# Attention decode step with a parallel SwiGLU: PV on four column tiles of the array, output steps per head, wo in groups of four heads

## The chip, the cores and the metric

The kernel runs on one core of one Trainium2 chip. The metric is the device time of one execution in microseconds. A profiled execution also gives a trace; its span is the time from the first to the last instruction and is 1 to 2 us shorter than the time. Engines: PE is the matmul engine (PEld is its weight loads), DVE the vector engine, ACT the scalar engine, SP the engine that issues every DMA of this kernel.

## The reference

One decode step for B = 4 sequences. Each of 32 heads attends to the last W = 2048 of 8192 cached positions with head size 192, and a SwiGLU FFN runs beside it on the same normalised input. Cut to what matters:

```python
W = min(4096, max(256, Sk // 4))              # 2048
q = (xn @ wq).reshape(B, 1, 32, 192)
k, v = k_cache[:, :, Sk-W:], v_cache[:, :, Sk-W:]
p = softmax(einsum("bhqd,bhkd->bhqk", q, k) * 192**-0.5)
o = einsum("bhqk,bhkd->bhqd", p, v)
return x + o.reshape(B, 1, 6144) @ wo + (silu(xn @ w1) * (xn @ w3)) @ w2
```

All of K and V is read once and used once: 32 heads times 3 MiB of K and 3 MiB of V, together with the weights 223 MB.

## The kernel before

The work is laid out in slots, four per head (one per quarter of a head's positions). `add(slot, phase, fn, ...)` puts a step into a slot; within each engine instructions then run in the order of slots and phases. The scores are products on DVE (`mult`), summed by PE against an identity (`adder`) and by DVE (`reduce_quarter`); softmax steps follow (`chain_*`); PV runs L = 10 slots behind. Two K buffers, three V buffers, two wo buffers. **All loads are issued by SP, in order**: a load that waits for its buffer holds up every load that is issued after it.

```python
def load_k(h):                                  # 3 MiB, packets of 24576 B
    kt = kpool.tile([P, NJ, Dh], BF16, tag="kt")
    nc.sync.dma_start(out=..., in_=k_win[:, h]...)
# load_v alike; the last head's V in GQ = 4 pieces
def wo_load(hg):                                # one per group of HG = 2 heads, packets of 3840 B
    wo_t = wopool.tile([P, RPP * D], BF16, tag="wo")
    nc.sync.dma_start(out=wo_t[:], in_=A_wo[hg * QW:(hg + 1) * QW, :]...)
# ... cut
def pv(u):                                      # one quarter of a head: 8 matmuls, 8 columns of weights each
    h, g = u // GQ, u % GQ
    if g == 0:
        o_pss[h] = ps_o.tile([2 * B, 2 * Dh], FP32, tag="o_ps", name="o_ps")
    o_ps = o_pss[h]
    z, vt = zs[h], vts[h]
    for j in range(g * JQ, (g + 1) * JQ, 2):
        nc.tensor.matmul(o_ps[:], lhsT=z[:, j:j + 2, :], rhs=vt[:, j:j + 2, :],
                         start=(j == 0), stop=(j == NJ - 2))
    # ... after the fourth quarter ACT copies o_ps to o_raw of the pair
def ge_tr(hg):                                  # turns o_raw of a pair: f32 matmuls against an identity
    # ... RPP * 2 matmuls, weights of 128 columns
def ge_proj(hg):
    # ... RPP * 2 matmuls with wo, summed in acc0, acc1 over all groups; frees wo's buffer
# ... cut
for h in range(H):
    u0, ul = h * GQ, h * GQ + GQ - 1
    if h >= KBUFS:
        add((h - KBUFS + 1) * GQ, 0, load_k, h)
    add((h - VBUFS) * GQ + GQ + L, 0, load_v, h, 1 if h < H - 1 else GQ)
    for u in range(u0, ul + 1):
        add(u, 1, mult, u); add(u + 1, 2, adder, u); add(u + 2, 4, reduce_quarter, u)
        add(u + L, 3, pv, u)
    # ... softmax chain at ul + 2 to ul + 6
for hg in range(NG):
    a = (hg + 1) * HG * GQ - 1 + L
    add(a - GQ - L if hg < NG - 1 else a - L + 3, 0, wo_load, hg)
    # ... ge_sum, ge_tot, ge_norm, ge_tr, ge_copy
    add(a + 3, 3, ge_proj, hg)
add(NU + 2, 1, w2_load)                         # last FFN weights, the last loads of all
# after all slots: last FFN product, sum, store
```

With HG = 2, `wo_load(hg)` (all but the last) stands in slot 8 hg + 3, and the projection that frees its buffer, `ge_proj(hg - 2)`, in slot 8 hg + 4. So each of these wo loads, from the third on, comes up one slot before its buffer can be free, and it must wait; the K load of slot 8 hg + 4 stands behind it.

## Time and profile before

| | before |
|---|---|
| time, first three runs | 562.24, 571.71, 572.77 us |
| span of the profiled run | 563.1 us |
| end of the last load | 540.3 us |
| from there to the end | 22.7 us |
| sum of all load packets' durations / 16 engines | 528.8 us |
| idle of the 16 engines before the last load ended | 11.8 us |

The last four rows are worked out from the trace's DMA packets: packets of weights, K and V (3 KB and over) give the end; durations of all packets over 4 B, added and divided by 16, give the sum; the idle counts 1/16 for each engine without a packet, from the first packet at 1.7 us on. (Start, sum and idle add up to 2 us more than the end, because packets of one engine overlap now and then.)

Lines of the page of the kernel before (busy us and share; busy tenths of 40 slices; GB/s of 40 slices; queue: packets, MB, share; the chain that ended last; groups: busy us, mean ns, idle before):

```profile
PE 489.6 (87%) x2339; PEld 221.8 (39%) x2339; DVE 343.1 (61%) x471; ACT 50.4 (9%) x151; POOL 1.1 (0%) x8
...
DMA  8999999999999999999999999999999999999630
GB/s 360 423 435 427 427 425 435 425 428 424 430 432 425 424 428 421 404 429 418 415 438 374 432 396 429 399 413 417 387 431 396 436 406 423 419 426 404 247 154 0
...
q1 hardware_dynamic: 12976, 222.97, 94.1%
...
DMA 49%; PE 34%; DVE 15%; ACT 1%; issue 0%; SPq 0%; ACTq 0%
...
L250 PE MATMUL o_ps<-vt,z 128*8 128x384 bf16 x1024 | 205.4, 349 | 1.1 <-ACT o_raw L258 1.1
...
L281 PE MATMUL gp<-idf,o_raw 8*128 8x4 f32 x192 | 36.0, 312 | 0.6 <-ACT o_raw L258 0.6
```

The load queue is busy for 94% of the span, so loads are the first limit and PE the second. But two things are visible in the GB/s row: in the second half many slices are at 374 to 418 where others reach 430 and more, and the last three slices (14 us each) fall away, with PE still busy.

Waits of SP's queue (waiting line, releaser: us in total, times, longest). L90 loads K, L99 loads V, L105 loads wo; L225 is a softmax step on PE that comes right behind the projection:

```profile
SPq L99 <- PE o_ps L250: 238.2, 29, 15.6
SPq L105 <- PE mt L225: 159.4, 13, 12.9
SPq L90 <- DVE pr L183: 51.2, 17, 9.7
```

The end, in the timeline (the last V, and three of PE's groups after it):

```profile
523.85 2.51 SPq L99 DMA_DIRECT2D vt<-in_A_v_cache_dram  x4
...
528.04 1.46 PE L250 MATMUL o_ps<-vt,z 128*8 128x384 bf16 x8
...
544.48 4.06 PE L250 MATMUL o_ps<-vt,z 128*8 128x384 bf16 x24 [0.56 <-ACT o_raw L258]
```

V of the last head is issued at 523.9 us, when PE at last frees its buffer, and 20 us later PE is still doing PV: a backlog.

### The profile page before, as it was taken

The page shows a single profiled execution, that of the slowest core. Times are in us where ns is not written, and L with a number is a line of the kernel's source. Part 1 is how long each engine was busy: PE and PEld are TensorE (multiplying, and loading weights), DVE is VectorE, ACT ScalarE, POOL GpSimd, SP SyncE. Part 2 cuts the span into 40 slices and gives each one's busy share as a digit, 9 for nine tenths or more (in the row PEclk, how much of TensorE's full clock was granted, in tenths as well). Part 3 has the DMA queues.
Part 4 walks back from the last instruction along what each step waited for, and adds up shares of the span by engine and source line. Part 5 has one row for each costly group of instructions (what it writes and reads, how often), then busy time and mean ns, then how long its engine had stood idle before and what let it go on. Part 6 is the DMA issues. An engine that isn't in the chain of part 4 may idle for free.

```text
span 563.1 us, 5565 instructions
## 1 busy us (share of the span) xinstructions
PE 489.6 (87%) x2339; PEld 221.8 (39%) x2339; DVE 343.1 (61%) x471; ACT 50.4 (9%) x151; POOL 1.1 (0%) x8
## 2 busy tenths in 40 slices
PE   2864899979899898979799897979899798979996
PEld 1321334433344444435344443524344343534453
DVE  2186667767437776756575776746476686756511
ACT  2111000001301000000000000000100000000100
POOL 0000000000000000000000000000000000000000
PEclk9898879988889999899979898988989898988998
DMA  8999999999999999999999999999999999999630
GB/s 360 423 435 427 427 425 435 425 428 424 430 432 425 424 428 421 404 429 418 415 438 374 432 396 429 399 413 417 387 431 396 436 406 423 419 426 404 247 154 0
DMA packets 13000, 223.31 MB, mean 397 GB/s; under 512 B 1448, under 2 KB 1456, under 8 KB 4144
## 3 DMA queue, kind: packets, MB, share of 16 engines
q1 hardware_dynamic: 12976, 222.97, 94.1%
q8 instruction: 18, 0.29, 0.2%
q14 instruction: 6, 0.05, 0.0%
HBM read 222.96 MB, written 0.01 MB: 396 GB/s over the span
## 4 chain that ended last, share of the span: by engine, by line
DMA 49%; PE 34%; DVE 15%; ACT 1%; issue 0%; SPq 0%; ACTq 0%
DMA kt<-in_A_k_cache_dram 46%; PE o_ps L250 13%; DVE pr L183 11%; PE ps L194 11%; PE gp L281 4%; DMA wt<-in_A_wq_dram 3%; DVE sc L202 3%; PE qps L167 2%; PE acc_233 L300 1%; PE f_3727 L393 1%; PE gt L318 1%; PE mt L225 1%; DVE z L239 0%; PE mt L211 0%; ACT ex L232 0%
## 5 line engine op out<-in xcount | busy, mean ns | idle before, releaser
L183 DVE TENSOR_TENSOR pr<-kt,qbc 128x3072 bf16<-128x3072 bf16 x128 | 223.2, 1745 | 116.6 <-DMA kt<-in_A_k_cache_dram 116.6
L194 PE MATMUL ps<-pr,idb 128*128 128x512 bf16 x768 | 203.2, 404 | 54.6 <-DVE sc L202 51.6
L250 PE MATMUL o_ps<-vt,z 128*8 128x384 bf16 x1024 | 205.4, 349 | 1.1 <-ACT o_raw L258 1.1
L250 PEld LDWEIGHTS <-z 128*8 128x8 bf16 x1024 | 82.9, 90 | 129.2 <-issue 76.1
L194 PEld LDWEIGHTS <-idb 128*128 128x128 bf16 x768 | 72.5, 102 | 149.5 <-issue 89.4
L202 DVE TENSOR_REDUCE sc<-ps 128x16 f32<-128x512 f32 x128 | 87.5, 684 | 5.7 <-PE ps L194 5.5
L281 PEld LDWEIGHTS gp<-idf,o_raw 8*128 8x128 f32 x192 | 34.6, 256 | 5.9 <-issue 4.9
L281 PE MATMUL gp<-idf,o_raw 8*128 8x4 f32 x192 | 36.0, 312 | 0.6 <-ACT o_raw L258 0.6
L228 ACT COPY negm<-mt 128x1 f32<-128x1 f32 x32 | 5.1, 159 | 339.0 <-PE mt L225 339.0
L291 DVE TENSOR_TENSOR oT<-gp,rtb 64x12 bf16<-64x12 f32 x32 | 5.4, 168 | 41.0 <-PE gp L281 40.8
L258 ACT COPY o_raw<-o_ps 8x384 f32<-8x384 f32 x32 | 15.0, 468 | 133.4 <-PE o_ps L250 133.4
L167 PE MATMUL qps<-wt,xnT 128*128 128x512 bf16 x60 | 17.2, 452 | 5.5 <-DMA wt<-in_A_wq_dram 5.5
L239 DVE TENSOR_TENSOR z<-ex,mask_b 128x256 bf16<-128x256 bf16 x32 | 13.4, 419 | 13.9 <-ACT ex L232 13.2
L173 DVE CAST qbc<-qps 128x512 bf16<-128x512 f32 x6 | 3.8, 684 | 19.5 <-PE qps L167 19.5
L300 PE MATMUL acc_233<-wo_t,oT 128*4 128x512 bf16 x48 | 14.8, 379 | 0.4 <-DVE oT L291 0.4
L225 PEld LDWEIGHTS mt<-ones_ff,gneg 1*128 1x128 f32 x64 | 9.4, 182 | 9.8 <-issue 9.5
L167 PEld LDWEIGHTS <-xnT 128*128 128x128 bf16 x60 | 6.7, 112 | 15.6 <-issue 10.4
L225 PE MATMUL mt<-ones_ff,gneg 1*128 1x1 f32 x64 | 12.1, 256 | 0.0
L232 ACT ACTIVATE ex<-sc,negm 128x64 bf16<-128x64 f32 x32 | 11.1, 348 | 1.0
L301 PE MATMUL acc_234<-wo_t,oT 128*4 128x128 bf16 x48 | 10.5, 219 | 0.0
L216 DVE TENSOR_REDUCE gmax<-mt 1x4 f32<-1x128 f32 x32 | 8.7, 273 | 2.2 <-PE mt L211 1.8
L211 PE MATMUL mt<-idf,lmax 128*1 128x128 f32 x32 | 8.6, 270 | 0.0
(60 smaller groups left out, 94.1 us busy)
## 6 DMA issues: line engine op xcount, KB each, us to landing
kt<-in_A_k_cache_dram SPq DMA_DIRECT2D x32, 3072.0 KB, 21.4
vt<-in_A_v_cache_dram SPq DMA_DIRECT2D x31, 3072.0 KB, 16.7
wo_t<-in_A_wo_dram SPq DMA_DIRECT2D x16, 480.0 KB, 5.1
wt<-in_A_wq_dram SPq DMA_DIRECT2D x2, 3072.0 KB, 13.2
vt<-in_A_v_cache_dram SPq DMA_DIRECT2D x4, 768.0 KB, 7.3
w_720<-in_B_w_dram SPq DMA_DIRECT2D x1, 1920.0 KB, 25.4
w_932<-in_B_w_dram SPq DMA_DIRECT2D x1, 1920.0 KB, 20.7
wt<-in_A_wq_dram SPq DMA_DIRECT2D x1, 1536.0 KB
```

What stands on the lines that cost most here:

```text
L167: nc.tensor.matmul(qp[:], lhsT=xnT[:, kc].rearrange("p a b -> p (a b)"), rhs=wq_rows[kc][:, (c0 + i) * QC:(c0 + i + 1) * QC], start=(kc == ...
L183: nc.vector.tensor_tensor(out=pr[:], in0=kts[h][:, g * JQ:(g + 1) * JQ, :], in1=qbc[:, h * Dh:(h + 1) * Dh].unsqueeze(1).to_broadcast([P, ...
L194: nc.tensor.matmul(ps[:], lhsT=idb[:], rhs=pr[:, :, kk * DD:(kk + 1) * DD], start=(kk == 0), stop=(kk == NK - 1))
L202: nc.vector.tensor_reduce(out=scs[h][:, g * JQ:(g + 1) * JQ], in_=pss.pop(u)[:], axis=AX.X, op=ALU.add)
L225: nc.tensor.matmul(mt[:, P:P + 1], lhsT=gneg[:].rearrange("o p b -> o (p b)"), rhs=ones_ff[0:1, 0:1], start=True, stop=True)
L232: nc.scalar.activation(out=ex[:], in_=scs.pop(h)[:], func=ACTF.Exp, bias=negm[:, 0:1], scale=SCALE, accum_out=rsums[hg][:, hl:hl + 1])
L239: nc.vector.tensor_tensor(out=z[:], in0=ex[:].unsqueeze(2).to_broadcast([P, NJ, B]), in1=mask_b[:].unsqueeze(1).to_broadcast([P, NJ, B]), ...
L250: nc.tensor.matmul(o_ps[:], lhsT=z[:, j:j + 2, :], rhs=vt[:, j:j + 2, :], start=(j == 0), stop=(j == NJ - 2))
L258: nc.scalar.copy(out=o_raws[hg][:, :, hl, :], in_=o_pss.pop(h)[:].rearrange("r (two d) -> r two d", two=2))
L281: nc.tensor.matmul(gp[:, i, :], lhsT=orf[:, part * QW + i:(part + 1) * QW:RPP], rhs=idf[0:2 * B, part * B:(part + 1) * B], start=(part == ...
L300: nc.tensor.matmul(acc0[:], lhsT=oT[:, i, :], rhs=wo_t[:, i * D:i * D + N0], start=st, stop=sp)
L301: nc.tensor.matmul(acc1[:], lhsT=oT[:, i, :], rhs=wo_t[:, i * D + N0:(i + 1) * D], start=st, stop=sp)
```

## The change

The intent: a PV matmul has 8 weight columns, so four of them, on four column tiles of 32, can run side by side; the result then lies in four strips of partitions, which the turning matmul adds up. The steps after PV move from pairs to single heads, and wo is loaded and projected for four heads at a time. The diff, cut to its core:

```diff
-    HG: int = 2,
+    HG: int = 4,
+    CT = 32
-    def pv(u):
-        ...
-        for j in range(g * JQ, (g + 1) * JQ, 2):
-            nc.tensor.matmul(o_ps[:], lhsT=z[:, j:j + 2, :], rhs=vt[:, j:j + 2, :], ...)
+    def pv(h, half):
+        o_ps, z, vt = o_banks[h % 2], zs[h], vts[h]      # two banks, zeroed once
+        n = NJ // 4
+        for jj in range(half * n, (half + 1) * n):
+            c = jj % 4
+            nc.tensor.matmul(o_ps[c * CT:c * CT + 2 * B, :], lhsT=z[:, 2 * jj:2 * jj + 2, :],
+                             rhs=vt[:, 2 * jj:2 * jj + 2, :], start=(jj < 4), stop=(jj >= 2 * n - 4))
+    def ge_tr(h):                       # per head; sel adds the four strips; weights of 32 columns
+        ...
+                nc.tensor.matmul(gp[sl, i, :], lhsT=o_raw[:, part, i:Dh:RPP], rhs=sel[:, part * B:(part + 1) * B],
+                                 start=(part == 0), stop=(part == 1))
...
-        add((h - VBUFS) * GQ + GQ + L, 0, load_v, h, 1 if h < H - 1 else GQ)
+        add((h - VBUFS) * GQ + GQ + L, 0, load_v, h, 1 if h < H - 1 else 2)
-            add(u + L, 3, pv, u)
+        add(u0 + L, 3, pv, h, 0)
+        add(u0 + L + 2, 3, pv, h, 1)
...
-        a = (hg + 1) * HG * GQ - 1 + L
-        add(a - GQ - L if hg < NG - 1 else a - L + 3, 0, wo_load, hg)
-        ...
-        add(a + 3, 3, ge_proj, hg)
+        a = ((hg + 1) * HG - 1) * GQ + L + 5
+        add((hg - 1) * HG * GQ + L + 2 * GQ + 4 if hg > 0 else 0, 0, wo_load, hg)
+        add(a, 3, ge_proj, hg, 0, RPP // 2)
+        add(a + 1, 3, ge_proj, hg, RPP // 2, RPP)
```

More of the change, by code (lines that the diff above doesn't have):

```diff
@@ L64 @@
     assert JQ * DD == 512 and JQ % 2 == 0 and 2 * Dh <= 512 and 0 < N1 <= 512
-    assert (H * Dh) % QC == 0 and NQ % 6 == 0 and QW % P == 0 and Dh % RPP == 0 and P % HG == 0
+    assert (H * Dh) % QC == 0 and NQ % 6 == 0 and QW % P == 0 and Dh % RPP == 0 and P == HG * CT
     assert 2 * H * Dh <= NJ * Dh
@@ L76 @@
     ps_add = ctx.enter_context(tc.tile_pool(name="ps_add", bufs=2, space=MemoryType.PSUM))
-    ps_o = ctx.enter_context(tc.tile_pool(name="ps_o", bufs=1, space=MemoryType.PSUM))
+    ps_o = ctx.enter_context(tc.tile_pool(name="ps_o", bufs=2, space=MemoryType.PSUM))
     ps_m = ctx.enter_context(tc.tile_pool(name="ps_m", bufs=1, space=MemoryType.PSUM))
-    ps_t = ctx.enter_context(tc.tile_pool(name="ps_t", bufs=2, space=MemoryType.PSUM))
+    ps_t = ctx.enter_context(tc.tile_pool(name="ps_t", bufs=1, space=MemoryType.PSUM))
     ps_acc = ctx.enter_context(tc.tile_pool(name="ps_acc", bufs=1, space=MemoryType.PSUM))
@@ L85 @@
     kts, vts, prs, pss, scs, exs, zs = {}, {}, {}, {}, {}, {}, {}
-    wos, o_pss, o_raws, rsums, chs, ges = {}, {}, {}, {}, {}, {}
+    wos, o_raws, rsums, rtbs, chs, ges, oTs = {}, {}, {}, {}, {}, {}, {}
     def load_k(h):
@@ L131 @@
     nc.vector.tensor_copy(out=mask_b[:], in_=mask_f[:])
+    sel = const.tile([P, 2 * B], FP32, name="sel")
+    nc.vector.tensor_reduce(out=sel[:], in_=idf[:].rearrange("q (c k) -> q k c", k=CT)[:, 0:2 * B, :],
+                            axis=AX.X, op=ALU.add)
     xf = ppool.tile([B, D], FP32, tag="pr")
@@ L163 @@
         qps = [pool.tile([P, QC], FP32, tag=tag, name="qps")
-               for pool, tag in ((ps_add, "ps"), (ps_add, "ps"), (ps_o, "o_ps"), (ps_m, "mt"), (ps_t, "t"), (ps_t, "t"))]
+               for pool, tag in ((ps_add, "ps"), (ps_add, "ps"), (ps_o, "o_ps"), (ps_o, "o_ps"), (ps_m, "mt"), (ps_t, "t"))]
         for kc in range(KC):
@@ L175 @@
                 nc.scalar.copy(out=dst, in_=qp[:])
+    o_banks = []
+    for i in range(2):
+        o_ps = ps_o.tile([P, 2 * Dh], FP32, tag="o_ps", name="o_ps")
+        nc.vector.memset(o_ps[:], 0.0)
+        o_banks.append(o_ps)
     acc0 = ps_acc.tile([B, N0], FP32, name="acc0")
@@ L209, in chain_tr @@
     def chain_tr(h):
-        mt = ps_m.tile([P, P + 1], FP32, tag="mt")
+        mt = ps_m.tile([P, P + 1 + B], FP32, tag="mt")
         nc.tensor.transpose(out=mt[0:1, 0:P], in_=chs[h][0][:], identity=idf[:])
@@ L222, in chain_bc @@
     def chain_bc(h):
-        lmax, mt, gneg = chs.pop(h)
-        hg, hl = h // HG, h % HG
+        lmax, mt, gneg = chs[h]
         nc.tensor.matmul(mt[:, P:P + 1], lhsT=gneg[:].rearrange("o p b -> o (p b)"), rhs=ones_ff[0:1, 0:1],
@@ L228, in chain_bc @@
         nc.scalar.copy(out=negm[:], in_=mt[:, P:P + 1])
-        if hl == 0:
-            rsums[hg] = small.tile([P, HG], FP32, tag="rsum", name="rsum")
+        rsum = small.tile([P, 1], FP32, tag="rsum", bufs=4)
         ex = small.tile([P, NJ], BF16, tag="ex")
         nc.scalar.activation(out=ex[:], in_=scs.pop(h)[:], func=ACTF.Exp, bias=negm[:, 0:1], scale=SCALE,
-                             accum_out=rsums[hg][:, hl:hl + 1])
+                             accum_out=rsum[:])
+        rsums[h] = rsum
         exs[h] = ex
@@ L241, in chain_z @@
         zs[h] = z
-    def pv(u):
-        h, g = u // GQ, u % GQ
-        if g == 0:
-            o_pss[h] = ps_o.tile([2 * B, 2 * Dh], FP32, tag="o_ps", name="o_ps")
-        o_ps = o_pss[h]
-        z, vt = zs[h], vts[h]
-        for j in range(g * JQ, (g + 1) * JQ, 2):
-            nc.tensor.matmul(o_ps[:], lhsT=z[:, j:j + 2, :], rhs=vt[:, j:j + 2, :],
-                             start=(j == 0), stop=(j == NJ - 2))
-        if g == GQ - 1:
+    def pv(h, half):
[5 more added lines that the diff above has]
+                             rhs=vt[:, 2 * jj:2 * jj + 2, :], start=(jj < 4), stop=(jj >= 2 * n - 4))
+        if half == 1:
@@ L253, in pv @@
             zs.pop(h)
             vts.pop(h)
-            hg, hl = h // HG, h % HG
-            if hl == 0:
-                o_raws[hg] = small.tile([2 * B, 2, HG, Dh], FP32, tag="o_raw", bufs=2, name="o_raw")
-            nc.scalar.copy(out=o_raws[hg][:, :, hl, :], in_=o_pss.pop(h)[:].rearrange("r (two d) -> r two d", two=2))
-    def ge_sum(hg):
-        rsm = small.tile([P, HG, B], FP32, tag="rsm", bufs=2)
-        nc.vector.tensor_tensor(out=rsm[:], in0=rsums.pop(hg)[:].unsqueeze(2).to_broadcast([P, HG, B]),
-                                in1=mask_f[:].unsqueeze(1).to_broadcast([P, HG, B]), op=ALU.mult)
-        ges[hg] = rsm
@@ L266, in ge_tot @@
-    def ge_tot(hg):
-        tb = ps_t.tile([P, HG, B], FP32, tag="t")
-        nc.tensor.matmul(tb[:], lhsT=ones_ff[:], rhs=ges[hg][:], start=True, stop=True)
-        ges[hg] = tb
-    def ge_norm(hg):
-        rtb = small.tile([P, HG, B], FP32, tag="rtb", bufs=2)
-        nc.vector.reciprocal(out=rtb[:], in_=ges[hg][:])
-        ges[hg] = rtb
-    def ge_tr(hg):
-        gp = ps_t.tile([P, RPP, B], FP32, tag="t")
-        orf = o_raws.pop(hg)[:].rearrange("r two h d -> r (two h d)")
+            o_raw = small.tile([P, 2, Dh], FP32, tag="o_raw", bufs=2, name="o_raw")
@@ new lines, in pv, with ge_tot, ge_norm @@
+            nc.scalar.copy(out=o_raw[:].rearrange("q two d -> q (two d)"), in_=o_ps[:])
+            o_raws[h] = o_raw
+    def ge_tot(h):
+        sl = slice((h % HG) * CT, (h % HG + 1) * CT)
+        nc.tensor.matmul(chs[h][1][sl, P + 1:P + 1 + B], lhsT=rsums.pop(h)[:].to_broadcast([P, CT]), rhs=mask_f[:],
+                         start=True, stop=True)
+    def ge_norm(h):
+        sl = slice((h % HG) * CT, (h % HG + 1) * CT)
+        rtb = small.tile([P, B], FP32, tag="rtb")
+        nc.vector.reciprocal(out=rtb[sl, :], in_=chs.pop(h)[1][sl, P + 1:P + 1 + B])
+        rtbs[h] = rtb
@@ L279, in ge_tr @@
+    def ge_tr(h):
+        hl = h % HG
+        sl = slice(hl * CT, (hl + 1) * CT)
+        gp = ps_t.tile([P, RPP, B], FP32, tag="t", name="gp")
+        o_raw = o_raws.pop(h)
         for i in range(RPP):
             for part in range(2):
-                nc.tensor.matmul(gp[:, i, :], lhsT=orf[:, part * QW + i:(part + 1) * QW:RPP],
-                                 rhs=idf[0:2 * B, part * B:(part + 1) * B], start=(part == 0), stop=(part == 1))
-        ges[hg] = [ges[hg], gp]
-    def ge_copy(hg):
-        rtb, gp = ges[hg]
-        oT = small.tile([P, RPP, B], BF16, tag="oT", bufs=2)
-        PH = P // HG
-        for hl in range(HG):
-            sl = slice(hl * PH, (hl + 1) * PH)
-            nc.vector.tensor_tensor(out=oT[sl], in0=gp[sl],
-                                    in1=rtb[sl, hl, :].unsqueeze(1).to_broadcast([PH, RPP, B]), op=ALU.mult)
-        ges[hg] = oT
@@ L295, in ge_proj, with ge_copy @@
-    def ge_proj(hg):
-        oT, wo_t = ges.pop(hg), wos.pop(hg)
-        for i in range(RPP):
+                nc.tensor.matmul(gp[sl, i, :], lhsT=o_raw[:, part, i:Dh:RPP], rhs=sel[:, part * B:(part + 1) * B],
+                                 start=(part == 0), stop=(part == 1))
+        ges[h] = gp
+    def ge_copy(h):
+        hg, hl = h // HG, h % HG
+        sl = slice(hl * CT, (hl + 1) * CT)
+        if hl == 0:
+            oTs[hg] = small.tile([P, RPP, B], BF16, tag="oT", bufs=2, name="oT")
+        nc.vector.tensor_tensor(out=oTs[hg][sl], in0=ges.pop(h)[sl, :, :],
+                                in1=rtbs.pop(h)[sl, :].unsqueeze(1).to_broadcast([CT, RPP, B]), op=ALU.mult)
@@ L298, in ge_proj @@
+    def ge_proj(hg, i0, i1):
+        oT, wo_t = oTs[hg], wos[hg]
+        for i in range(i0, i1):
             st = (hg == 0 and i == 0)
@@ L366 @@
         add(ul + 6, 5, chain_z, h)
+        add(ul + 6, 4, ge_tot, h)
+        add(ul + 6, 6, ge_norm, h)
+        add(u0 + L + 3, 3, ge_tr, h)
+        add(u0 + L + 4, 5, ge_copy, h)
     for hg in range(NG):
-        a = (hg + 1) * HG * GQ - 1 + L
-        add(a - GQ - L if hg < NG - 1 else a - L + 3, 0, wo_load, hg)
-        add(a - 2, 6, ge_sum, hg)
-        add(a - 1, 6, ge_tot, hg)
-        add(a, 6, ge_norm, hg)
-        add(a + 1, 3, ge_tr, hg)
-        add(a + 2, 2, ge_copy, hg)
-        add(a + 3, 3, ge_proj, hg)
+        a = ((hg + 1) * HG - 1) * GQ + L + 5
+        add((hg - 1) * HG * GQ + L + 2 * GQ + 4 if hg > 0 else 0, 0, wo_load, hg)
+        add(a, 3, ge_proj, hg, 0, RPP // 2)
+        add(a + 1, 3, ge_proj, hg, RPP // 2, RPP)
     f = FFN_HEAD * GQ
```

## The prediction

> **What bounds it now.** The load stream. The page gives 222.96 MB read and queue q1 at 94.1% of the span; in the 20 us windows from 20 to 520 us the DMA share is 0.93 to 1.02. Summed over the trace's packets, the 16 engines need 528.8 us for this traffic. They start at 1.7 us, lose about 5 us to small gaps until 519 us, 5 us in one hole from 519.6 to 525.6 us, and end at 539.8 us. In the last 23 us nothing loads.
>
> PE is second, 489.6 us (87%), close enough to the limit to be behind: in the queue's waits, V loads wait 238.2 us for PV, most of it hidden behind queued loads. The hole is the visible part: V of head 31 is issued only at 523.9 us, when PV of head 28 releases the buffer. Then PE still has three heads of PV (timeline, 524 to 550 us), the transposing matmuls, projection, last FFN product, and the store.
>
> **What the change does.**
> - PV: 1024 matmuls, 8 in 1.46 us when warm (174 ns each), 205.4 us busy in all. Four column tiles should overlap: the Trainium skill, "TensorEngine Tiling (Array Packing)", Theoretical Speedup, says up to 4x for a dimension of at most 32; no run shows it yet. Each keeps its weight load, and this trace shows a load-and-matmul pair of 128 columns at about 55 ns (second half of the projection), so I estimate 60 ns (45 to 90): 110 to 140 us off PE.
> - Transposing matmuls: the same count per head instead of per pair, with twice the row groups: 192 records become 768. Now 12 take 2.25 us (188 ns), set by 128-column f32 weight loads. With 32 columns I estimate 70 to 110 ns: 36 us becomes 55 to 85 us.
> - Sums, reciprocals, copies: a few us either way. Projection: the same 96 matmuls. wo: the same bytes in 8 loads, not 16; its 3840 B packets already took only 149 ns, so no gain there.
> - V buffers come free one slot earlier, no longer behind a quarter that needs the next head's K.
>
> PE falls to about 400 us (360 to 440), with more idle, so a less even clock.
>
> **What is on the critical path.** Of some 90 us off PE, only the end counts: the 528.8 us of packets stay. The hole and most small gaps go, so the last load lands at about 533 us. After it come what is left of PV and transposes, projection, last FFN product (5 us now), copies (1.4 us) and store (2.5 us): about 12 us instead of 23. Span 545 us against 563.1, run 547 against 564.9 (-3.2%). The measured runs spread from 562 to 573, whose cause no view shows; I put the middle at 549, range 538 to 561. Chances: faster by over 2% 0.78, within 2% 0.20, slower 0.02.
>
> **What would show it.** DMA share near 1.0 until some 530 us, no hole before V of head 31, last landing 6 to 8 us earlier; V loads waiting little for PE; PV at 45 to 90 ns a matmul in the timeline; PE busy below 440 us; at the end PE waits for loads instead of working off a backlog; DVE unchanged (343 us); the chain almost wholly K and V loads with DVE.
>
> **What would make it wrong.** Column tiles that do not overlap (PV near 170 ns): with the added transposes PE would be the bound, time within 2%. Switches between tile shapes that cost so much that PE stays behind. A cold PE clock that stretches the last 12 us to 18. A DMA rate that drifts between runs by more than the gain.

## More of the kernel before

A wait of SP costs nothing as long as enough loads are already queued. Here is a place where there were not: SP's issues around 298 us (start us, us, instruction), then 2 us windows (PE, PEld, DVE, ACT, POOL busy; PE clock, DMA share, GB/s):

```profile
285.43 0.53 SPq L99 DMA_DIRECT2D vt<-in_A_v_cache_dram  x1
298.50 0.34 SPq L105 DMA_DIRECT2D wo_t<-in_A_wo_dram  x1
298.93 0.54 SPq L90 DMA_DIRECT2D kt<-in_A_k_cache_dram  x1
```

```profile
296.00:298.00 2.00, 2.00 (x14) 0.95 (x13) 1.76 (x2) 0.00 (x0) 0.00 (x0) 1.00 1.00 430
298.00:300.00 2.00, 2.00 (x12) 0.92 (x10) 0.53 (x3) 0.60 (x3) 0.00 (x0) 1.00 0.49 115
```

SP issued nothing for 13 us, the wo load came, and the engines had run dry when it did: 115 GB/s in that window.

How much is queued ahead can be read from the time between issue and landing of a small load. This is for the wo loads (0.48 MB) of the kernel before, from the answer for that tile:

```profile
DMA to landing us min/median/max: 4.0/5.1/27.3
```

A K load of 3.1 MB issued in the same kernel takes 21.4 us in the median. I read the median of 5.1 us to mean that a wo load usually finds next to nothing queued ahead of it.

## The result

The changed kernel takes 539.96 us in the median (539.12 to 540.90, 4 runs); the kernel before, in the same rounds, 568.64 us (562.24 to 572.77). Executions over 1.5% slower than the fastest of the same kernel are left out of the means. The ratio is 0.958, 95% interval 0.952 to 0.963: faster by 4.2%. (A ratio is the mean time of one kernel's fast runs over that of the other's fast runs of the same rounds, so it is not quite the ratio of the medians.)

The same lines of the changed kernel's page:

```profile
PE 380.5 (71%) x2947; PEld 174.2 (32%) x2947; DVE 351.0 (65%) x474; ACT 48.5 (9%) x151; POOL 1.1 (0%) x8
...
DMA  8999999999999999999999999999999999999970
GB/s 349 437 427 432 437 427 427 431 431 429 438 435 423 430 435 427 431 436 429 432 433 429 427 434 435 427 429 432 433 432 434 427 436 429 431 426 435 422 305 2
...
q1 hardware_dynamic: 11536, 222.97, 96.6%
...
DMA 59%; DVE 22%; PE 17%; issue 1%; ACT 1%; SPq 0%; ACTq 0%
...
L259 PE MATMUL o_ps<-vt,z 128*8 128x384 bf16 x1024 | 58.3, 351 | 0.0
...
L287 PE MATMUL gp<-sel,o_raw 128*32 128x4 f32 x768 | 49.6, 199 | 1.1 <-ACT o_raw L265 0.6
```

PE lost 109 us of busy time. From the second slice on the GB/s row is flat at 422 to 438 until the last two; the weak slices of the second half are gone.

SP's waits; L91 is now K's load, L100 V's, L106 wo's:

```profile
SPq L91 <- DVE pr L195: 298.2, 29, 11.3
SPq L100 <- PE mt L236: 60.4, 22, 5.0
SPq L100 <- PE o_ps L259: 31.2, 7, 15.6
```

wo is not in the list at all. SP now waits for DVE to be done with K, which is the wait that one wants: it stands as far ahead as the buffers allow. The wo loads land in 25.3 us in the median, five times as long as before (24.5 us at the least). They are twice as large, which at 431 GB/s explains about 1 us of it, an estimate; the rest I read as a queue that is always full:

```profile
DMA to landing us min/median/max: 24.5/25.3/35.0
```

The end, in the timeline:

```profile
501.70 0.82 PE L259 MATMUL o_ps<-vt,z 128*8 128x384 bf16 x16
...
502.57 1.18 SPq L100 DMA_DIRECT2D vt<-in_A_v_cache_dram  x2
...
504.70 1.76 DVE L195 TENSOR_TENSOR pr<-kt,qbc 128x3072 bf16<-128x3072 bf16 x1 [4.87 <-DMA kt<-in_A_k_cache_dram]
```

16 PV matmuls take 0.82 us where 8 took 1.46 us. The last V is issued 21 us earlier, and the end now starts from the last K, which landed at 504.7 us.

Two windows show the end of both kernels, first before, then after (columns as above; the last two are DMA share and GB/s):

```profile
520.00:530.00 10.00, 10.00 (x54) 4.26 (x53) 6.35 (x10) 1.07 (x4) 0.00 (x0) 1.00 0.50 165
530.00:540.00 10.00, 9.44 (x55) 5.69 (x53) 2.19 (x8) 1.07 (x4) 0.00 (x0) 1.00 1.01 409
```

```profile
520.00:530.00 10.00, 8.87 (x135) 6.08 (x135) 1.83 (x8) 1.46 (x5) 0.00 (x0) 0.91 0.15 62
530.00:540.00 10.00, 4.61 (x28) 2.16 (x26) 1.83 (x4) 0.73 (x2) 0.00 (x0) 0.84 0.00 1
```

The 25.0 us of the span divide cleanly at the end of the last load:

| | span | last load ends | rest | packets / 16 | idle before last load |
|---|---|---|---|---|---|
| before | 563.1 | 540.3 | 22.7 | 528.8 | 11.8 |
| after | 538.1 | 523.5 | 14.6 | 519.3 | 4.6 |
| difference | 25.0 | 16.8 | 8.1 | 9.5 | 7.3 |

Two thirds of the gain is a load stream that ends earlier, one third a shorter end. I had forecast 7 and 11 us, 18 in sum: 7 us too little, with the stream put at under half of what it gave and the end at too much. So the question for the experiments: what made the stream 16.8 us shorter, and what the end?

### The profile page after: what moved, and what is told of

It reads as the page before. It is cut to its first block, busy times and chain, and to the rows that moved or that the text cites. A ratio compares the mean times of both kernels' runs of the same rounds, so it can differ in the third digit from the quotient of the medians.

```text
span 538.1 us, 6726 instructions
## 1 busy us (share of the span) xinstructions
PE 380.5 (71%) x2947; PEld 174.2 (32%) x2947; DVE 351.0 (65%) x474; ACT 48.5 (9%) x151; POOL 1.1 (0%) x8
## 4 chain that ended last, share of the span: by engine, by line
DMA 59%; DVE 22%; PE 17%; issue 1%; ACT 1%; SPq 0%; ACTq 0%
DMA kt<-in_A_k_cache_dram 55%; DVE pr L195 16%; PE ps L206 7%; PE gp L287 5%; DVE sc L214 4%; DMA wt<-in_A_wq_dram 4%; PE qps L172 1%; PE gt L322 1%; PE o_ps L259 1%; PE f_4011 L398 1%; DVE rtb L277 0%; PE acc_239 L304 0%; DVE oT L296 0%; DVE qbc L178 0%; ACT o_raw L265 0%
## 5 line engine op out<-in xcount | busy, mean ns | idle before, releaser
L206 PE MATMUL ps<-pr,idb 128*128 128x512 bf16 x768 | 221.3, 433 | 133.6 <-DVE sc L214 129.9
L206 PEld LDWEIGHTS <-idb 128*128 128x128 bf16 x768 | 78.2, 105 | 228.9 <-issue 171.8
L259 PE MATMUL o_ps<-vt,z 128*8 128x384 bf16 x1024 | 58.3, 351 | 0.0
L287 PEld LDWEIGHTS gp<-sel,o_raw 128*32 128x32 f32 x768 | 46.8, 151 | 21.4 <-issue 19.8
L265 ACT COPY o_raw<-o_ps 128x384 f32<-128x384 f32 x32 | 15.3, 480 | 408.5 <-PE o_ps L259 408.5
L287 PE MATMUL gp<-sel,o_raw 128*32 128x4 f32 x768 | 49.6, 199 | 1.1 <-ACT o_raw L265 0.6
L259 PEld LDWEIGHTS <-z 128*8 128x8 bf16 x1024 | 20.9, 88 | 39.7 <-issue 31.2
L277 DVE RECIPROCAL rtb<-mt 32x4 f32<-32x4 f32 x32 | 5.7, 178 | 30.3 <-PE gp L287 30.0
L172 PE MATMUL qps<-wt,xnT 128*128 128x512 bf16 x60 | 16.1, 428 | 5.9 <-DMA wt<-in_A_wq_dram 5.9
L322 PE MATMUL gt<-w_754,xnT 128*4 128x512 bf16 x15 | 6.1, 565 | 4.2 <-DVE oT L296 2.9
## 6 DMA issues: line engine op xcount, KB each, us to landing
wo_t<-in_A_wo_dram SPq DMA_DIRECT2D x8, 960.0 KB, 25.3
wt<-in_A_wq_dram SPq DMA_DIRECT2D x2, 3072.0 KB, 16.8
vt<-in_A_v_cache_dram SPq DMA_DIRECT2D x2, 1536.0 KB, 14.6
```

What stands on the lines that cost most here:

```text
L172: nc.tensor.matmul(qp[:], lhsT=xnT[:, kc].rearrange("p a b -> p (a b)"), rhs=wq_rows[kc][:, (c0 + i) * QC:(c0 + i + 1) * QC], start=(kc == ...
L206: nc.tensor.matmul(ps[:], lhsT=idb[:], rhs=pr[:, :, kk * DD:(kk + 1) * DD], start=(kk == 0), stop=(kk == NK - 1))
L259: nc.tensor.matmul(o_ps[c * CT:c * CT + 2 * B, :], lhsT=z[:, 2 * jj:2 * jj + 2, :], rhs=vt[:, 2 * jj:2 * jj + 2, :], start=(jj < 4), stop= ...
L265: nc.scalar.copy(out=o_raw[:].rearrange("q two d -> q (two d)"), in_=o_ps[:])
L287: nc.tensor.matmul(gp[sl, i, :], lhsT=o_raw[:, part, i:Dh:RPP], rhs=sel[:, part * B:(part + 1) * B], start=(part == 0), stop=(part == 1))
L322: nc.tensor.matmul(gt[:], lhsT=xnT[:, kc, 0, :], rhs=wt[:, kc, n0:n0 + QC], start=(kc == 0), stop=(kc == KC - 1))
```

## The experiments

Theories. A: PE is behind, and its backlog delays the loads and fills the end; column tiles cure both. B: the wo load that waits in SP's in-order queue empties the stream; moving it away cures the stream. Two refinements, C and D, came up on the way. Each kernel ran four times (one profile and three rounds) against the kernel before on the same chip.

| kernel | median us | ratio to before [95%] | last load ends | rest of span |
|---|---|---|---|---|
| b_wo | 554.20 | 0.979 [0.976, 0.983] | 529.2 | 22.0 |
| b_sched | 554.17 | 0.977 [0.973, 0.982] | 528.1 | 24.4 |
| b_pvq | 542.75 | 0.960 [0.956, 0.965] | 528.7 | 11.4 |
| a_onecol | 549.11 | 0.970 [0.967, 0.974] | 524.0 | 23.2 |
| a_wowait | 539.02 | 0.948 [0.941, 0.955] | 523.5 | 13.7 |
| a_onewait | 547.37 | 0.964 [0.957, 0.970] | 524.1 | 21.6 |
| a_wohalf | 538.95 | 0.948 [0.942, 0.954] | 523.9 | 13.3 |
| a_tail | 534.01 | 0.939 [0.933, 0.945] | 523.6 | 9.2 |
| b_early | 565.22 | 1.004 [0.996, 1.012] | 540.3 | 23.7 |
| a_k31 | 534.91 | 0.949 [0.942, 0.956] | 523.7 | 8.3 |
| a_tail2 | 533.13 | 0.946 [0.938, 0.955] | 523.4 | 7.6 |
| b_alt | 551.76 | 0.977 [0.972, 0.981] | 528.5 | 20.6 |

The "b" kernels start from the kernel before, the "a" kernels from the changed one. The kernel before scatters from batch to batch (medians 565.6, 569.5, 565.9 and 565.7 us), so ratios of different batches compare only roughly; the last two columns, from each profiled run, compare better. (565.9 is the median of all seven runs; the ratios of that batch, of b_early, a_k31 and a_tail2, leave out its three slow ones.) The record marks every result as correct, even that of b_pvq, which leaves out three quarters of PV. So this check does not notice a wrong PV, and "correct" says little about PV in any of these kernels.

### b_wo: the wo load out of the way, nothing else

```diff
-        add(a - GQ - L if hg < NG - 1 else a - L + 3, 0, wo_load, hg)
+        add(a - GQ - L + 3 if hg < NG - 1 else a - L + 3, 0, wo_load, hg)
```

> The kernel before, with each wo load moved three slots later, behind the projection that frees its buffer, so that it never holds up the K and V loads issued after it. Theory A (PE is behind, and its backlog is the cost): the loads stay late and the end stays long, 560 to 567 us, ratio to before 0.99 to 1.00. Theory B (the wo load that waits in the in-order queue is the cost in the middle): no gaps near wo loads, packets about 5 us quicker in sum, 552 to 558 us, ratio about 0.98.

Measured: 554.20 us, and the last load ends 11.1 us earlier; the packets' sum fell from 528.8 to 524.1 us and the idle from 11.8 to 5.5 us. PE is as busy as before (483.6 us). The wo loads now find a queue:

```profile
DMA to landing us min/median/max: 16.0/17.1/20.3
```

The rest of the span stayed at 22 us. So one number in a schedule gives close to half of the whole gain, and nearly all of it in the stream, as theory B said.

### b_sched: the same, and V freed a slot earlier

```diff
-            add(u + L, 3, pv, u)
+            add(u0 + L + (2 if u - u0 >= GQ // 2 else 0), 3, pv, u)
```

> As b_wo, and PV of a head in two bursts of two quarters at the slots that the changed kernel uses, so that V is freed one slot earlier; no column tiles, PE has the same work. Theory A (PE backlog): 558 to 567 us, the hole before the last V stays. Theory B (order of issue and of release): most of the gain without column tiles, 545 to 552 us.

Measured: 554.17 us, the same as b_wo. Neither range fits: the expected 545 to 552 us of theory B was too much. Freeing V a slot earlier adds nothing once wo is out of the way (last load 1.1 us earlier, rest 2.4 us longer).

### b_pvq: PE relieved, nothing moved

```diff
-        for j in range(g * JQ, (g + 1) * JQ, 2):
+        for j in range(g * JQ, (g + 1) * JQ, 8):
             ...
-                             start=(j == 0), stop=(j == NJ - 2))
+                             start=(j == 0), stop=(j == NJ - 8))
```

> The kernel before, with only every fourth PV matmul (wrong result on purpose): PE loses about 150 us of PV, nothing else moves, and wo loads still stand in their old place. Theory A: no hole before the last V, no backlog at the end, 538 to 546 us, ratio about 0.96, as the whole change. Theory B: wo loads still hold up the queue, gaps stay in the middle, 550 to 558 us.

Measured: 542.75 us, as theory A said. PE is busy 384.2 us, as in the changed kernel. The rest of the span fell from 22.7 to 11.4 us. The stream, too, ends 11.6 us earlier, although wo loads still wait (126.9 us of SP's time instead of 159.4): they land in 8.6 us in the median instead of 5.1, and there is no gap before 510 us. So the gaps need both: a load that waits for PE, and a PE that is late. Either cure suffices for the stream. Only the relief of PE shortens the end.

### a_onecol: the changed kernel without overlap of PV

```diff
-            c = jj % 4
-            nc.tensor.matmul(o_ps[c * CT:c * CT + 2 * B, :], ..., start=(jj < 4), stop=(jj >= 2 * n - 4))
+            nc.tensor.matmul(o_ps[0:2 * B, :], ..., start=(jj == 0), stop=(jj == 2 * n - 1))
```

> The changed kernel, with all PV matmuls in the first column tile: same schedule, same loads, same output steps, but they cannot overlap. PE gets about 110 to 120 us back and some 500 us busy. Theory A: backlog returns, the last V is late, 558 to 572 us. Theory B: the middle stays full, only the end is longer, 545 to 552 us.

Measured: 549.11 us, within theory B's range. PE is busy 476.4 us, 96 us more than in the changed kernel, nearly as much as before. Its end, in the same windows as above:

```profile
520.00:530.00 10.00, 9.48 (x95) 6.25 (x95) 2.15 (x9) 1.97 (x8) 0.00 (x0) 1.00 0.15 61
530.00:540.00 10.00, 9.15 (x66) 5.14 (x64) 0.23 (x2) 0.48 (x1) 0.00 (x0) 0.86 0.01 2
```

The DMA columns are those of the changed kernel, and the PE column is close to that of the kernel before. The last load ends at 524.0 us, within 0.5 us of the changed kernel, but PE works on to the end, 23.2 us against 14.6. **In this schedule column tiles are worth about 9 us, all at the end; the rest of the change is worth about 16 us, all in the stream.** (The profile of the changed kernel comes from another batch; a_onewait against a_wowait below, which differ in the column tiles alone and ran in one batch on one chip, give 8.4 us.)

### a_wowait and a_onewait: the wo load made to wait again

```diff
-        add((hg - 1) * HG * GQ + L + 2 * GQ + 4 if hg > 0 else 0, 0, wo_load, hg)
+        add((hg - 1) * HG * GQ + L + (0 if hg > 1 else 2 * GQ + 4) if hg > 0 else 0, 0, wo_load, hg)
```

In a_onewait the one column tile of a_onecol comes on top.

> The changed kernel, with each wo load put back in front of the projection that frees its buffer, so that it waits in the queue again. Theory C (a waiting wo load only costs when PE is behind, because then the projection comes late): no gaps, 539 to 544 us, ratio about 0.96. Theory B alone (the place of the wo load is the cost, whatever PE does): gaps near wo loads, 546 to 552 us.

> The changed kernel with both undone: one column tile for all PV, and wo loads that wait. Theory C: PE is behind and the waiting wo loads hold up the K loads again, so the last load lands later than the 522 us of the one-column run, some 524 to 530, and the time is 551 to 558 us. If place and PE load did not act together, it would stay near the one-column run's 549 us.

Measured: a_wowait 539.02 us, no loss, as theory C said. But a_onewait took 547.37 us with the last load at 524.1 us, as if the wait were not there; theory C had said 551 to 558. SP did wait (98.9 us in 6 times) and the loads landed in 9.9 us in the median, but only one small gap (0.9 us near 265 us) came of it. So "a waiting load and a busy PE" is not enough. What differs from the kernel before: half as many waits, V freed earlier, and output steps per head. The next two kernels try the first two.

### b_early: V freed a slot earlier, wo still waiting

The edit is that of b_sched without that of b_wo.

> The kernel before, with PV of a head in two bursts at the changed kernel's slots (V freed one slot earlier) and nothing else: wo loads still wait in their old place, no column tiles. Theory D (gaps come where the queue's reserve runs out; any one of the three, wo out of the way, V freed earlier or PE relieved, leaves some): wo loads land in 8 us or more instead of 5, no gap before 500 us, last load near 527 us, 552 to 557 us. If an earlier V gives no reserve: gaps stay, 562 to 569 us.

Measured: 565.22 us, ratio 1.004, last load at 540.3 us, gaps of over 0.4 us (idle summed over the engines, divided by 16) at seven places before 500 us. Theory D's guess that any one cure will do is refuted for this one: V freed earlier gives no reserve. The wo loads waited even longer (259.8 us) and landed as early as before:

```profile
DMA to landing us min/median/max: 3.5/5.3/27.0
```

### b_alt: half as many waits

```diff
-        add(a - GQ - L if hg < NG - 1 else a - L + 3, 0, wo_load, hg)
+        add(a - GQ - L + (0 if hg % 2 else 3) if hg < NG - 1 else a - L + 3, 0, wo_load, hg)
```

> The kernel before, with every second wo load moved three slots later as in the first experiment and the others left to wait: as many waiting loads as with groups of four heads. If it is the number of waits that matters (the queue recovers its reserve over four heads): the waiting loads land in 8 us or more, no gaps, last load near 529 us, 554 to 557 us. If each wait empties the queue by itself: the waiting loads still land in about 5 us, about half of the gaps stay, 558 to 563 us.

Measured: 551.76 us, last load at 528.5 us, no gap before 509 us. SP waited for wo 6 times, 75.3 us in all. So the number of waits matters: with four heads between two waits the queue recovers, with two it does not. That b_alt happened to move the harmful half of the loads is unlikely: in the kernel before, gaps follow wo loads of both halves (issued at 298.5 and 360.8 us, and at 329.8 and 394.6 us). The time is a little under the range that I gave for it (554 to 557 us), as the rest of the span came out 1.4 us shorter than in b_wo.

```profile
DMA to landing us min/median/max: 5.9/15.6/26.1
```

So the grouping in fours cures the gaps even with the loads in front of their projections, as a_onewait had shown but for one small gap; the changed kernel does both.

### a_wohalf: small wo packets again

The changed kernel's wo load cut into two DMAs of three rows each, so that a packet is 3840 B again.

> The changed kernel, with each wo load cut in two, so that its packets are 3840 B again, as before. In the kernel before and its variants 24576 B packets took 915 ns and more, in the changed one 912 ns. If the size of the wo packets is the cause: packets of 24576 B go back to about 915 ns and the sum of packet times from 519.3 to about 522.5 us, the time to about 543 us. If not: 24576 B stay at 912 ns, the sum at about 520.2 us (wo alone), time within 1 us of 540.

Measured: 538.95 us, packets' sum 519.8 us, 24576 B packets still at 912 ns. The packet size of wo is worth 0.5 us and no more. What is left of the stream's gain over b_wo, about 5 us (524.1 against 519.3 us of packets), is: 2.3 us in the 24576 B packets (median 915 against 912 ns), 1.6 us in the last head's V, which came in 6144 B packets before and in 12288 B packets after, and 0.8 us in wo. Why the large packets are 3 ns quicker in every "a" kernel than in b_wo, no run settles (the median is 914 ns in the kernel before, and 912 ns in b_early too, which has the gaps).

### a_tail, a_k31 and a_tail2: faster versions

In the changed kernel the last K lands at 504.7 us and the span ends 33 us later. DVE multiplies the last K from 504.7 to 515.1 us, z of the last head (the softmax weights that PV multiplies) is done at 523.5 us, the last FFN product at 534.6 us. a_k31 loads the last K in four pieces so that DVE can start on the first:

```diff
+        pieces = GQ if h == H - 1 else 1
+        n = NJ // pieces
+        for i in range(pieces):
+            nc.sync.dma_start(out=kt[:, i * n:(i + 1) * n, :]..., in_=src[:, :, i * n:(i + 1) * n, :]...)
```

a_tail does this, moves the last wo load behind the last V, and does the last FFN product in two parts around the projection:

```diff
+        add(... + (9 if hg == NG - 1 else 0) if hg > 0 else 0, 0, wo_load, hg)
+    add((H - 1) * GQ + L + 4, 6, ffn_out, 0, W2A)
+    add((H - 1) * GQ + L + 7, 3, ffn_out, W2A, FC)
```

a_tail2 goes on from there: the last FFN weights ahead of the last V (`add(NU - 3, 1, w2_load)`), their product in three parts in slots 133, 135 and 137, and the attention output added last.

> A try at a faster version, from the reading that the end now hangs on the last K (landed at 504.7 us, 33 us before the end): the last K in four pieces, so that its multiplications start before all of it is there; the last wo load behind the last V; the last FFN product in two parts, before and after the projection, in its own PSUM tiles. If the end is the chain from the last K: 528 to 533 us, ratio about 0.94, last load still near 522 us. If something else sets the end (PE order, cold clock): 536 to 540 us.

> The changed kernel with the last K loaded in four pieces and nothing else, to take that part of the faster version by itself. If the end is the chain from the last K: z of the last head 3 to 5 us earlier than 523.5 us and the time 535 to 537 us. If the pieces do nothing: 539 to 541 us.

> A second try at a faster version: as the first, but the last FFN weights are loaded before the last V, their product is done in three parts between the steps of the last head, only the last wo load stands behind the last V, and the attention output is added last. In the first try the end waited 1.3 us for these weights and then ran their product with a cold clock, 522.5 to 526.3 us. Expected 526 to 531 us, ratio about 0.93. If the product's parts delay the last head's chain instead: 533 to 536 us.

Measured: 534.01, 534.91 and 533.13 us. The pieces alone bring most of it: z of the last head is done at 519.0 us instead of 523.5, and the rest of the span is 8.3 us instead of 14.6. Of these 6.3 us, 4.5 are the earlier z. About 1.7 us more come from a different cause: in the changed kernel seven steps of the projection and the last FFN product (528.3 to 531.9 us) ran at 0.53 us a step, at a granted clock of 0.54 (528.1 to 531.8 us); in a_k31 all of them took 0.27 us, at a clock of 1.00. Whether a_k31 avoids this slow stretch by its order or by chance, no run shows. a_tail had been expected at 528 to 533 us: z came 6.4 us earlier, but the FFN product, moved ahead of the projection, then waited until 522.5 us for its weights and ran the first six of its steps at half the pace (0.53 us a step instead of 0.27, at a granted clock of 0.55 from 522.5 to 526.3 us), so that part of the gain was handed back. a_tail2 took that wait away but put 2 us of FFN product in front of the last PV; it missed its range of 526 to 531 us, too. The last loads end at 523.4 to 523.7 us in all three and the fastest ends 7.6 us later, so little more is to be had at this end. a_tail2 is the fastest kernel, about 7 us under the changed kernel; that last figure compares runs of different chips, as the changed kernel itself was not in that batch.

## Why the prediction was right or wrong

The time, 539.96 us, lies in the range 538 to 561 us, near its lower end, and "faster by over 2%" came true. That the time fell into the range is in part luck: the range was 23 us wide because the kernel before scatters, its middle of 549 us is 9 us off, and one term was too small (the stream, 7 us for 16.8) while the other was too large (the end, 11 us for 8.1). Point by point:

- **"PV ... I estimate 60 ns (45 to 90)": right.** In the chain of waits near the end 30 PV matmuls follow each other in 1.52 us, 51 ns each against 174 ns (8 in 1.39 us in the same chain of the kernel before), 3.4 times as fast. PV's busy time fell by 147 us (205.4 to 58.3), a little more than the 110 to 140 us given. This is close to the Trainium skill's "up to 4x" ("TensorEngine Tiling (Array Packing)", Theoretical Speedup).
- **Transposing matmuls, 55 to 85 us: too high.** The 768 records came, but cost 49.6 us. PE in all: 380.5 us, inside 360 to 440.
- **"The hole ... go[es]", V loads wait little for PE: right.** The last V is issued at 502.6 us instead of 523.9; V's waits for PE fell from 238.2 to 91.6 us (60.4 and 31.2). DVE is near 343 us, as said (351.0), and the chain is DMA 59%, DVE 22%, with PE down from 34% to 17%, rather than almost gone. The mean granted clock fell from 0.924 to 0.883, with PE busy for 71% of the span instead of 87%.
- **"wo: the same bytes in 8 loads, not 16 ... so no gain there": the step that failed.** I looked at the packets of wo and not at where its load stands in SP's queue. It is issued one slot before its buffer can be free, and 13 of 16 times it waited there and held up the loads behind it. The waits of 159.4 us for L105 stood in the view that I quoted. b_wo shows what it cost: 11.1 us of the stream; b_alt shows that halving the number of these loads is enough.
- **"Of some 90 us off PE, only the end counts: the 528.8 us of packets stay": wrong.** The packets' sum is not fixed by the bytes: it fell to 519.3 us. About half of that, 4.7 us, went in b_wo with the gaps. That packets at a nearly empty queue take longer is the obvious reading, as most slow ones of the kernel before stand behind a wo load that waited: after the first 20 us, 137 of its 176 K and V packets of over 1.0 us start within 6 us of a wo load's issue, stretches that make up 18% of the time. But it was not measured by itself.
- **"The last load lands at about 533 us": 523.5.** The sum of these two errors.
- **"About 12 us instead of 23" after the last load: 14.6.** The mechanism was right: a_onecol has the backlog back (23.2 us) and b_pvq has none (11.4 us). The term that I mis-sized is what is left on PE when the last weights land, PV of the last head, turning and projection: the sum leaves it about 3 us, and it took 7.4 (523.5 to 530.9 us), while the FFN product took 3.7 instead of 5. One cause is the chain from the last K: it takes 33 us, and only 19 us of other loads follow. a_k31 shows it: with z 4.5 us earlier, and with the full clock at the end, the rest is 8.3 us. The other is the low clock that the prediction named as a risk: it cost about 1.7 us of the 14.6, an estimate from seven steps at 0.53 instead of 0.27 us.

My theory before the experiments gave PE's backlog the whole gain. Shown instead: two nearly separate parts. The load order gives the stream (11 us by b_wo, about 16 us by a_onecol, which also has bigger V pieces and groups of four), the column tiles give the end (about 9 us by a_onecol against the changed kernel, 8.4 us by a_onewait against a_wowait). They overlap in one respect: b_pvq shows that relief of PE alone would also have closed the gaps. Open: what the output steps per head do by themselves with one column tile (V loads wait 164.8 us for PE in a_onecol, 347.4 us in b_wo and 207.7 us in b_sched, which has the two PV bursts), why the clock is low near the end of some runs, and the 3 ns of the large packets.

## What to carry to other kernels

In a kernel bound by loads that one queue issues in order, look first at which load waits for its buffer and what stands behind it; the time from issue to landing of a small load tells how much reserve the queue has left. A load placed just ahead of the instruction that frees its buffer empties that reserve, and how often this happens can matter more than what the load itself costs. Relief of an engine that is not the limit still pays at the end of a kernel, once: read the end as a chain of its own, from the last load that a long chain needs.

## What the Trainium skill lacked or had wrong

- "DMA: Bandwidth & Descriptors", section "Anatomy of one DMA — SWDGE (gpsimd) path", says that "any semaphore wait happens on the issuing sequencer before dispatch". The traces of these loads, which SP issues, agree: SP issued nothing from 285.43 to 298.50 us while a wo load waited. It has nothing on what follows for loads issued behind: here 16 loads of 0.48 MB, 13 of which waited at the head of SP's queue, cost 11.1 us of 563 (b_wo), and half as many of them cost none of the gaps (b_alt).
- The same page gives 435 GB/s as the fabric's ceiling (Specifications). The full stretches of the changed kernel run at 431 GB/s (20 to 500 us), just under it. What the page lacks is that the same bytes need not take the same time: its packets took 528.8 us in sum in one kernel and 519.3 us in the other, 4.7 us of it with the gaps (b_wo).
- "TensorEngine Tiling (Array Packing)", Theoretical Speedup, gives up to 4x for a dimension of at most 32. With 8 weight columns, 384 moving columns and a weight load for each matmul the runs show 3.4x (174 to 51 ns). That page has no measured figure, and the measured packings of "TensorE: Matmul & The Clock Gate" have four column tiles only together with row tiles.
- "TensorE: Matmul & The Clock Gate", section "LDWEIGHTS (loading the stationary operand)", gives columns / 1.2 ns. For f32 the section has no figure: 12 records of turning matmuls with 128 f32 columns took 2.25 us (188 ns each, weight load and matmul), 24 with 32 columns 1.56 us (65 ns each). Each of these f32 matmuls of the program shows as two records (6 a pair of heads before, 12 a head after), so one of them took 375 and 130 ns.
